# Attention and a mixture of adapters: three score buffers, two shared PSUM banks, casts tied to VectorE steps

## The chip, the cores and the metric

One core of one Trainium2 chip runs the whole kernel. The metric is the device time of one execution in microseconds (us). Engines are named as in the profile: PE is TensorE, DVE is VectorE, ACT is ScalarE, POOL is GpSimd, and SP is SyncE, which here only issues DMAs.

## The reference

Eight batches of eight heads, 576 positions, head size 64. Scores get a bias that depends on the distance of query and key; softmax; then values. The result x, 4608 rows of 512, goes through a gated mixture of eight adapters of rank 16, the best two per row.

```python
scores = scale * np.matmul(q, k.transpose(0, 1, 3, 2))
scores = scores + bias.transpose(2, 0, 1)[None]     # bias_table[bucket(|i - j|)]
attn = np.exp(scores - scores.max(-1, keepdims=True))
attn = attn / (attn.sum(-1, keepdims=True) + 1e-09)
x = np.matmul(attn, v)                              # then rows of all heads side by side
logits = x @ w_gate
w = softmax over the best two logits of a row
out = x + sum over those two e of w[e] * ((x @ A[e]) @ B[e])
```

## The kernel before, in words

The work goes in 32 pairs of heads (`i`, four pairs `hp` per batch `b`). Of the 576 positions 512 are the main part, in four tiles of 128, and 64 are a tail; the tails of the two heads of a pair share one tile. A pair has five score groups `g`: groups 0 to 3 are a key tile against the 512 main queries, for both heads, and group 4 has the tails.

`qk(i, g)` (L316) takes a `sc` tile (two PSUM banks, two buffers), runs the score matmuls (L323, or L327 and L331 for group 4), and has ACT write `exp` of them as bf16 into `p` (L335). The bias comes in as a factor: `band` (L338) multiplies the parts of `p` near the diagonal by exp of the bias, from `M` or `M4`; two heads by 256 or 384 columns at L350 (shown as 128x512 and 128x768), 256 columns at L342 for group 4. `pv(i, sl)` (L355) multiplies all groups with the values for one of five slots of 128 query rows, with a column of ones for the sum. All five slots stand in one tile `pv` of two banks, which has one buffer. `norm` (L380) takes the reciprocal of the sums (L388), a mask for the tail slot (L391), and multiplies 640 columns into `x` (L392).

Ahead of that, `cast_kq` (L122) makes bf16 copies `kqn` of keys and queries, and `cast_v` (L134) of values `vn`, on POOL. `transposes` (L281) turns `kqn` by eight PE transposes into `kqps`, and DVE copies that to `kqT` (L289). The mixture of a batch (`m_*`, L401 to L538) follows its attention: x transposed by a DMA on SP (`m_xdma`, L404), logits (L438), gates on DVE, POOL and ACT (`m_gate`), z (L487), its transpose (L505), outputs (L513), a sum on DVE (L517) and stores on SP (L523, L538). The shared tail tile of two batches has instructions of its own. All PSUM tiles but `sc` and `pv` take turns in two one-bank buffers named `acc`.

The order on every engine is written out by hand. The loop (L587 to L632) goes through pairs and, inside, groups: the scores of group `g` of pair `i`; then transposes for pair `i+1`, mixture steps that `mixture` (L543) has put into `events` at a group's number, values of pair `i-1`, its norm at group 4; and last the band of the group before (`late`). Each engine runs its own instructions in that order. SP takes, in the same order, loads of the next batch (`load_kq`, `load_v`), stores and the transposing DMA. POOL takes tail loads (`load_tails`, `load_vtails`), casts and gate steps. Before the loop (L139 to L255) come the loads of batch 0, with values cast by 16 DMAs from POOL (L152), and the bias: a row `g_sb` made on DVE, its exp `ge` (L189), written to DRAM (L191) and read back as shifted copies `Mr` and `MHr` (L198, L204), from which `bias_pair` (L221) builds `M`, `M4` and `MHT`.

Of the kernel before, what the change touches and what calls it, by code (L numbers as in the profile page):

```python
# [10 lines left out]
FP32 = mybir.dt.float32  # L11
# [16 lines left out]
def kernel(  # L28
# [37 lines left out]
    scp = ctx.enter_context(tc.tile_pool(name="sc_ps", bufs=2, space=PSUM))  # L66
    pvp = ctx.enter_context(tc.tile_pool(name="pv_ps", bufs=1, space=PSUM))
# [3 lines left out]
    make_identity(nc, ident)  # L71

# [3 lines left out]
    def alloc_loads(b):  # L76
        kf = ldp.tile([128, H, 4 * D], FP32, name="kf", tag="kf")
        qf = ldp.tile([128, H, 4 * D], FP32, name="qf", tag="qf")
        kfs[b] = (kf, qf)
        if b > 0:  # L80
            vfs[b] = ldp.tile([128, 4, H, D], FP32, name="vf", tag="vf")
# [25 lines left out]
    def load_tails(b):  # L107
        for w, src in enumerate((k, q)):
            sr = src[b, :, S4:, :].rearrange("(c e) p d -> e p c d", e=2)
            for e in range(2):  # L110
                s = slice(e * 64, (e + 1) * 64)
                nc.gpsimd.dma_start(out=tls[b % 2][s, w, :, s], in_=sr[e])

    def load_vtails(b):
        sr = v[b, :, S4:, :].rearrange("(c e) p d -> e p c d", e=2)
        for e in range(2):
            nc.gpsimd.dma_start(  # L117
                out=vts[b % 2][e * 64:(e + 1) * 64, :, e * D1:e * D1 + D], in_=sr[e])
# [3 lines left out]
    def cast_kq(i, w, eng=None):  # L122
# [8 lines left out]
        else:  # L131
            (eng or nc.gpsimd).tensor_copy(o, s)  # L132

    def cast_v(i):  # L134
        b, hp = divmod(i, HP)
        h = slice(2 * hp, 2 * hp + 2)
        nc.gpsimd.tensor_copy(vns[b % 2][:, :, h, :D], vfs[b][:, :, h, :])  # L137

    alloc_loads(0)  # L139
    load_kq(0, 0, 2)  # L140
    btT = cp.tile([H, NB], FP32, tag="btT")
    nc.sync.dma_start(out=btT, in_=bias_table.rearrange("b h -> h b"))
    for t in tls[:1] + vts[:1]:
        nc.vector.memset(t, 0.0)
    load_kq(0, 2, 4)
    load_kq(0, 4, 6)
    load_tails(0)

    nc.vector.memset(vns[0][:, :, :, D:D1], 1.0)
    for j in range(4):  # L150
        for t in range(4):
            nc.gpsimd.dma_start(  # L152
                out=vns[0][j * 32:(j + 1) * 32, t, :, :D],
                in_=v[0, :, t * 128:(t + 1) * 128, :]
                .rearrange("h (p j) d -> j p h d", j=4)[j])
# [5 lines left out]
    nc.vector.memset(g_sb, 0.0)  # L161
    cast_kq(0, 0, nc.vector)
    cast_kq(0, 1, nc.scalar)
    bsub = cp.tile([H, NB], FP32, tag="bsub")
    nc.vector.tensor_scalar(bsub, btT, btT[:, NB - 1:NB], None, op0=ALU.subtract)
# [11 lines left out]
    nc.vector.tensor_copy(g_sb[:, C:C + nsm], bsub[:, :nsm])  # L177
    nc.vector.tensor_copy(
# [3 lines left out]
    for bv, lo, hi in runs[nsm:]:  # L182
# [3 lines left out]
        nc.vector.tensor_copy(dst, bsub[:, bv:bv + 1].unsqueeze(2)  # L186
# [4 lines left out]
    nc.sync.dma_start(out=g_d.ap(), in_=ge)  # L191
# [42 lines left out]

    for t in tls[1:] + vts[1:]:
# [430 lines left out]
```

## Time and profile before

| What | Value |
|---|---|
| Runs | 254.53, 255.85, 285.35 us; median 255.85 |
| Profiled execution | 256.31 us, span 254.5 us |
| PE busy | 187.8 us (74%) |
| DVE busy | 195.0 us (77%) |
| ACT busy | 162.7 us (64%) |
| POOL busy | 117.3 us (46%) |
| Mean granted clock of PE | 0.919 |

The span is the time from the first to the last instruction; what lies around it is not in the profile. Busy shares are means over the span. PE's matmuls are pipelined and overlap in the records, so a busy PE need not be at its peak. In rows of time, the first number is the start and the second the duration, in us, and what stands in brackets is the idle time just before and what ended it. Rows with merged instructions carry a count (x8) and the time from the first start to the last end.

### The profile page before, as it was taken

What the parts mean: (1) busy time and instruction counts of PE and PEld (TensorE: products, weight loads), DVE (VectorE), ACT (ScalarE), POOL (GpSimd) and SP (SyncE); (2) the same over time, 40 slices, a digit from 0 to 9 for tenths busy, and PEclk for the clock granted to TensorE, in tenths of its full rate; (3) what the DMA queues carried; (4) which work ended last, traced back from release to release, by engine and by line L of the source; (5) the groups of instructions that cost most, each with busy time, mean ns of one, the idle gap of its engine ahead of it and who ended that gap; (6) DMA issues with size and microseconds to landing.
All of it is one profiled execution on the core that took longest, in us unless ns stands there. A gap on an engine that the chain in (4) does not pass through costs nothing.

```text
span 254.5 us, 6519 instructions
## 1 busy us (share of the span) xinstructions
PE 187.8 (74%) x2496; PEld 123.7 (49%) x2496; DVE 195.0 (77%) x483; ACT 162.7 (64%) x184; POOL 117.3 (46%) x229
## 2 busy tenths in 40 slices
PE   1324965888987596869879898879784997897650
PEld 1102543655754473546646574547353675556510
DVE  5215673899999579897997698988998599798771
ACT  3251874689987485777876586769676487895000
POOL 8599928671835254334743282714452282020100
PEclk9999998899999889899997797999889599999965
DMA  7999996997988697596987693886967301910616
GB/s 163 148 128 271 273 97 146 308 150 153 322 108 199 135 292 113 128 186 157 324 155 166 166 304 38 183 175 198 244 152 162 74 0 38 213 45 3 165 36 170
DMA packets 91830, 41.28 MB, mean 162 GB/s; under 512 B 69648, under 2 KB 87064, under 8 KB 91800
## 3 DMA queue, kind: packets, MB, share of 16 engines
q1 hardware_dynamic: 74392, 38.77, 61.5%
q0 software_dynamic: 17408, 2.10, 14.8%
q8 instruction: 19, 0.31, 0.5%
q14 instruction: 11, 0.09, 0.1%
HBM read 29.84 MB, written 9.45 MB: 154 GB/s over the span
## 4 chain that ended last, share of the span: by engine, by line
PE 43%; DVE 32%; DMA 13%; POOL 7%; issue 2%; ACT 1%; DVEq 0%; POOLq 0%; ACTq 0%
PE pv L366 17%; DMA xT<-x 11%; PE sc L323 9%; DVE p L350 6%; DVE x L392 6%; DVE o L517 5%; PE zp L487 3%; DVE p L342 3%; DMA tl<-in_q_dram 3%; DVE rm L391 3%; PE dl L513 3%; PE kqps L287 3%; DVE kqT L289 2%; POOL vn L152 2%; DVE tlT L298 2%
## 5 line engine op out<-in xcount | busy, mean ns | idle before, releaser
L335 ACT ACTIVATE p<-sc 128x1024 bf16<-128x1024 f32 x160 | 155.8, 1024 | 65.7 <-PE sc L323 36.1
L366 PE MATMUL pv<-vn,p 128*128 128x65 bf16 (+1 forms) x1152 | 68.2, 206 | 12.6 <-DVE x L392 12.5
L366 PEld LDWEIGHTS <-p 128*128 128x128 bf16 x1280 | 59.0, 104 | 37.4 <-issue 18.9
L350 DVE TENSOR_TENSOR p<-p,M 128x512 bf16<-128x512 bf16 (+1 forms) x128 | 66.2, 533 | 3.3 <-POOL M L223 2.7
L323 PE MATMUL sc<-kqT 64*128 64x512 bf16 x256 | 54.0, 419 | 2.8 <-ACT p L335 2.8
L287 PE MATMUL kqps<-ident,kqn 128*128 128x128 bf16 x256 | 21.6, 229 | 17.0 <-POOL kqn L132 10.0
L366 PE MATMUL pv<-vt,p 128*128 128x130 bf16 x128 | 29.8, 232 | 2.4 <-DVE p L342 2.4
L453 POOL TENSOR_TENSOR df<-lg,m 128x32 f32<-128x32 f32 (+1 forms) x12 | 3.5, 293 | 60.6 <-DVE lg L443 31.8
L287 PEld LDWEIGHTS <-kqn 128*128 128x128 bf16 x256 | 15.8, 101 | 24.6 <-POOL kqn L132 11.3
L392 DVE TENSOR_TENSOR x<-pv,rm 128x640 bf16<-128x640 f32 x32 | 26.4, 825 | 1.1
L289 DVE COPY kqT<-kqps 128x1024 bf16<-128x1024 bf16 x32 | 21.8, 682 | 7.0 <-PE kqps L287 7.0
L117 POOL DMA_DIRECT2D vt<-in_v_dram x16 | 9.8, 621 | 32.6 <-PE pv L366 32.6
L517 DVE TENSOR_TENSOR o<-dl,x 128x512 f32<-128x512 f32 x32 | 21.7, 687 | 3.7 <-PE dl L513 2.7
L323 PEld LDWEIGHTS <-kqT 64*128 64x128 bf16 x256 | 12.8, 94 | 18.5 <-issue 7.3
L132 POOL CAST kqn<-kf 128x512 bf16<-128x512 f32 x31 | 21.1, 680 | 0.1
L132 POOL CAST kqn<-qf 128x512 bf16<-128x512 f32 x31 | 20.5, 662 | 0.0
L137 POOL CAST vn<-vf 128x512 bf16<-128x512 f32 x28 | 20.5, 733 | 0.0
L342 DVE TENSOR_TENSOR p<-p,M 128x256 bf16<-128x256 bf16 x32 | 18.5, 579 | 0.1
L513 PE MATMUL dl<-Bb,zT 128*128 128x512 bf16 x32 | 14.2, 452 | 4.4 <-DVE kqT L289 2.5
L327 PE MATMUL sc<-kqT,tlT 128*128 128x512 bf16 x32 | 13.7, 427 | 0.0
L331 PE MATMUL sc<-tlT,kqT 128*128 128x128 bf16 x128 | 13.5, 233 | 0.0
L438 PE MATMUL lp<-Wb,xT 128*128 128x8 bf16 x128 | 4.5, 167 | 11.9 <-DMA xT<-x 11.9
(85 smaller groups left out, 209.3 us busy)
## 6 DMA issues: line engine op xcount, KB each, us to landing
out_dram<-o SPq DMA_DIRECT2D x64, 128.0 KB, 2.3
kf<-in_k_dram SPq DMA_DIRECT2D x7, 1024.0 KB, 5.9
qf<-in_q_dram SPq DMA_DIRECT2D x7, 1024.0 KB, 10.2
vf<-in_v_dram SPq DMA_DIRECT2D x112, 64.0 KB, 2.9
kf<-in_k_dram SPq DMA_DIRECT2D x4, 256.0 KB, 4.5
qf<-in_q_dram SPq DMA_DIRECT2D x4, 256.0 KB, 4.4
out_dram<-ot SPq DMA_DIRECT2D x8, 128.0 KB, 2.6
tl<-in_k_dram POOLq DMA_DIRECT2D x16, 32.0 KB, 6.8
```

What stands on the lines that cost most here:

```text
L132: (eng or nc.gpsimd).tensor_copy(o, s)
L137: nc.gpsimd.tensor_copy(vns[b % 2][:, :, h, :D], vfs[b][:, :, h, :])
L287: nc.tensor.transpose(o[:, :, j, :], n[:, w, j], ident)
L289: nc.vector.tensor_copy(t, ps)
L323: nc.tensor.matmul(sc[:, h * 512:(h + 1) * 512], lhsT=t[s, 0, g * 128:(g + 1) * 128], rhs=t[s, 1, :], start=True, stop=True)
L335: nc.scalar.activation(p, sc, ACT.Exp, scale=scale)
L342: nc.vector.tensor_tensor(p[:, 384:640], p[:, 384:640], M4[:, hp, :], op=ALU.mult)
L350: nc.vector.tensor_tensor(o, o, Mh[:, :, x0 * 128:(x0 + b1 - b0) * 128], op=ALU.mult)
L366: nc.tensor.matmul(acc[:, sl * SLOT + o:sl * SLOT + o + n], lhsT=lhsT, rhs=rhs, start=start, stop=stop, skip_group_check=True)
L392: nc.vector.tensor_tensor(xs[b][:, :, 2 * hp:2 * hp + 2, :], at(acc, 0, (SLOT, 5), (D1, 2), (1, D)), rm.unsqueeze(3).to_broadcast((128, 5, ...
L513: nc.tensor.matmul(ps, lhsT=zT[:, t, :], rhs=Bb, start=True, stop=True)
L517: nc.vector.tensor_tensor(o[:, t], ps, xs[b][:, t].rearrange("p h d -> p (h d)"), op=ALU.add)
```

## The change

- Score tiles `sc` get three buffers. `qk` only runs matmuls, for group number n (five per pair, counted through); the activation is a function `expo(n)`. The loop issues scores two groups ahead: `qk(n + 2)`, then `expo(n)`.
- The `pv` pool goes. `pv` takes a one-bank `acc` tile for slots 0 to 2 and another for slots 3 and 4. `norm` has two parts, at groups 2 and 4, with a reciprocal each (`recip`); the mask step is two slots wide.
- All DVE instructions go through a `Recorder` that keeps the last one. `behind_dve` makes a POOL cast wait for the last DVE instruction issued before it. In the loop the three casts of a pair stand just ahead of a DVE step that reads PSUM: the copy of `kqT` at group 0, and the two parts of `norm` at groups 2 and 4.
- Head: the bias table is loaded first; batch 0's values are loaded as fp32 by ACT's and SP's queues, and cast on DVE; `ge` is written by ACT's queue; casts for pairs 0 to 2 and bias tiles for pairs 0 and 1 are on DVE. Tail loads are issued one piece at a time.
- Mixture weights are loaded and cast by POOL's DMAs, without POOL casts. Value loads for the next batch go in 2, 1 and 1 pieces at pairs 0, 1 and 2 of a batch.
- Mixture: the tail tile becomes a fifth tile of `xT` and of all steps after it in every second batch; steps are placed at other groups (`mixture`).

```diff
-    scp = ctx.enter_context(tc.tile_pool(name="sc_ps", bufs=2, space=PSUM))
-    pvp = ctx.enter_context(tc.tile_pool(name="pv_ps", bufs=1, space=PSUM))
+    scp = ctx.enter_context(tc.tile_pool(name="sc_ps", bufs=3, space=PSUM))
     acp = ctx.enter_context(tc.tile_pool(name="acc_ps", bufs=2, space=PSUM))
...
+    dve = Recorder(nc.vector)
+
+    def behind_dve(inst):
+        tc.add_manual_dep(
+            inst.ins, dve.last.ins.name,
+            mybir.DependencyInfo(mybir.DependencyClass.Sync,
+                                 mybir.DependencyReason.DATA),
+            reason="reads SBUF beside an instruction with an input in PSUM")
...
     alloc_loads(0)
-    load_kq(0, 0, 2)
     btT = cp.tile([H, NB], FP32, tag="btT")
     nc.sync.dma_start(out=btT, in_=bias_table.rearrange("b h -> h b"))
+    load_kq(0, 0, 2)
+    load_v(0, (0, 1), nc.scalar)
...
+    for w in range(2):
+        for e in range(2):
+            load_tail(0, w, e)
     load_kq(0, 2, 4)
+    load_v(0, (2, 3))
     load_kq(0, 4, 6)
-    load_tails(0)
...
-            nc.gpsimd.dma_start(
-                out=vns[0][j * 32:(j + 1) * 32, t, :, :D],
...
-    nc.sync.dma_start(out=g_d.ap(), in_=ge)
+    nc.scalar.dma_start(out=g_d.ap(), in_=ge)
+    cast_kq(0, 0, dve)
+    cast_kq(0, 1, nc.scalar)
+    cast_kq(1, 0, dve)
+    cast_kq(1, 1, dve)
...
+        k = sl % 3
+        if k == 0:
+            pvs[(i, sl // 3)] = acp.tile([128, 3, 2 * D1], FP32, name="pv", tag="acc")
...
+    def recip(i, part):
+        if i % HP == 0 and part == 0:
+            xs[i // HP] = xp.tile([128, 5, H, D], BF16, name="x", tag="x", bufs=4)
+        n = 3 - part
+        rc = sp.tile([128, n, 2], FP32, name="rc", tag=f"rc{part}")
+        dve.reciprocal(rc, at(pvs[(i, part)], D, (2 * D1, n), (D1, 2)))
+        rcs[(i, part)] = rc
...
         if b < B - 1:
-            at_slot(0, 0, lambda: m_xdma(b))
+            at_slot(0, 4, m_xdma, b)
         else:
+            at_slot(0, 4, m_x, b, 0)
+            at_slot(0, 4, m_x, b, 1)
+        if tail:
+            at_slot(1, 4, m_xtail, b)
+        at_slot(2, 0, m_logits, b)
+        for n in range(4):
+            at_slot(2, (2, 3, 4, 4)[n], m_gate, b, n)
+        at_slot(3, 0, m_z, b, 0, 4)
+        if tail:
+            at_slot(3, 2, m_z, b, 4, 5)
+        at_slot(3, 4, m_zT, b)
+        at_slot(4, 0, m_out, b, 0)
+        at_slot(4, 2, m_out, b, 1)
+        at_slot(5, 0, m_out, b, 2)
+        at_slot(5, 2, m_out, b, 3)
+        if tail:
+            at_slot(6, 4, m_outt, b)
...
+    for n in range(NG + 5):
+        i, g = divmod(n, 5)
         b, hp = divmod(i, HP)
+        nb = b + 1
+        if n + 2 < NG:
+            qk(n + 2)
+        if n < NG:
+            expo(n)
...
+            for j in ((0, 1), (2,), (3,), ())[hp]:
+                load_v(nb, (j,))
+        if g in (1, 3) and hp < 3 and nb < B:
+            load_tail(nb, hp, g // 2)
+        if 10 <= n < 15:
+            load_weights(n - 10)
...
+        if i < HP and g == 2:
+            cast_v(i, dve)
+        if n == 2:
+            bias_pair(0, dve)
+            band(0)
+        if g == 4 and i > 0:
+            mask_tail(i - 1)
+        if 1 < n <= NG:
+            band(n - 1)
...
+        if g == 0 and i + 1 < NPAIR:
+            if 3 <= i + 2 < NPAIR:
+                behind_dve(cast_kq(i + 2, 0))
+            transposes(i + 1)
+        if g == 2 and hp == 2 and nb < B:
+            tail_transposes(nb)
+        if i > 0:
+            if g == 1:
+                pv(i - 1, 0)
+                pv(i - 1, 1)
+            if g == 2:
+                pv(i - 1, 2)
+                recip(i - 1, 0)
+            if g == 3:
+                pv(i - 1, 3)
+                pv(i - 1, 4)
+                recip(i - 1, 1)
+        if g == 2 and 3 <= i + 2 < NPAIR:
+            behind_dve(cast_kq(i + 2, 1))
+        if g == 4 and HP <= i + 1 < NPAIR:
+            behind_dve(cast_v(i + 1))
+        if i > 0 and g in (2, 4):
+            norm(i - 1, g // 2 - 1)
+        for f, a in events.pop(n, ()):
+            f(*a)
```

## Rows read from the trace of the kernel before

**Rows 1.** Windows: us, busy (x) of PE, PEld, DVE, ACT, POOL; clock; DMA share.

```profile
0.00:25.60 25.60, 7.69 (x45) 3.68 (x45) 8.95 (x38) 7.98 (x11) 21.45 (x50) 1.00 1.09 178
25.60:233.50 207.90, 170.13 (x2333) 114.04 (x2332) 173.93 (x413) 154.29 (x172) 94.60 (x174) 0.93 0.77 165
233.50:254.50 21.00, 10.03 (x120) 5.97 (x120) 12.17 (x34) 0.44 (x2) 1.30 (x6) 0.75 0.42 113
```

**Rows 2.** Timeline of PE, the first matmul of group 4 of four pairs.

```profile
95.25 0.38 PE L327 MATMUL sc<-kqT,tlT 128*128 128x512 bf16 x1
104.42 0.38 PE L327 MATMUL sc<-kqT,tlT 128*128 128x512 bf16 x1
225.95 0.38 PE L327 MATMUL sc<-kqT,tlT 128*128 128x512 bf16 x1
230.97 0.38 PE L327 MATMUL sc<-kqT,tlT 128*128 128x512 bf16 x1
```

**Rows 3.** Timeline of SP's queue and PE, x transposed and used.

```profile
136.46 1.80 SPq L404 DMA_TRANSPOSE xT<-x  x1
140.95 0.55 PE L438 MATMUL lp<-Wb,xT 128*128 128x8 bf16 x16 [1.30 <-DMA xT<-x]
```

**Rows 4.** Timeline of DVE, POOL and PE in one long pair.

```profile
96.06 1.87 DVE L350 TENSOR_TENSOR p<-p,M 128x768 bf16<-128x768 bf16 x1
96.84 0.66 POOL L132 CAST kqn<-kf 128x512 bf16<-128x512 f32 x1
98.31 0.61 PE L287 MATMUL kqps<-ident,kqn 128*128 128x128 bf16 x8 [1.30 <-DVE zT L507]
100.26 0.38 PE L513 MATMUL dl<-Bb,zT 128*128 128x512 bf16 x1 [0.96 <-DVE kqT L289]
```

**Rows 5.** Windows, a stretch behind those waits.

```profile
101.00:103.00 2.00, 2.00 (x14) 0.77 (x12) 1.63 (x4) 1.02 (x1) 0.00 (x0) 0.50 0.00 0
```

**Rows 6.** Waits: engine line <- releaser: us in total, times, longest us.

```profile
PE pv L366 <- DVE x L392: 12.5, 13, 1.9
```

**Rows 7.** DVE instructions of three lines: duration in ns, min/median/max.

```profile
L342 DVE TENSOR_TENSOR p<-p,M x32: 279/283/2512, 25.6 to 233.5; 128x256 bf16<-128x256 bf16 x32
L391 DVE TENSOR_TENSOR rm<-rc,mask x32: 152/164/1953, 32.0 to 236.7; 128x10 f32<-128x10 f32 x32
L392 DVE TENSOR_TENSOR x<-pv,rm x32: 824/825/826, 32.6 to 236.9; 128x640 bf16<-128x640 f32 x32
```

**Rows 8.** Groups by form, whole span: xcount | busy us, mean ns | idle.

```profile
L350 DVE TENSOR_TENSOR p<-p,M 128x768 bf16<-128x768 bf16 x64 | 38.4, 609 | 0.6 <-ACT p L335 0.5
L350 DVE TENSOR_TENSOR p<-p,M 128x512 bf16<-128x512 bf16 x64 | 29.3, 458 | 2.7 <-POOL M L223 2.7
L342 DVE TENSOR_TENSOR p<-p,M 128x256 bf16<-128x256 bf16 x32 | 18.5, 579 | 0.1
L391 DVE TENSOR_TENSOR rm<-rc,mask 128x10 f32<-128x10 f32 x32 | 10.2, 319 | 0.0
L388 DVE RECIPROCAL rc<-pv 128x10 f32<-128x10 f32 x32 | 6.8, 212 | 7.2 <-PE pv L366 7.1
```

**Rows 9.** Groups by form, DVE, 226 to 254.5 us, almost without casts.

```profile
L350 DVE TENSOR_TENSOR p<-p,M 128x768 bf16<-128x768 bf16 x3 | 1.6, 548 | 0.0
L350 DVE TENSOR_TENSOR p<-p,M 128x512 bf16<-128x512 bf16 x3 | 1.1, 374 | 0.0
```

**Rows 10.** Timeline of PE with queued work.

```profile
117.06 0.41 PE L366 MATMUL pv<-vn,p 128*128 128x65 bf16 x8
117.36 0.38 PE L327 MATMUL sc<-kqT,tlT 128*128 128x512 bf16 x1
118.18 0.39 PE L323 MATMUL sc<-kqT 64*128 64x512 bf16 x2
```

**Rows 11.** Timeline of the head, SP's queue and POOL.

```profile
12.86 1.75 SPq L198 DMA_DIRECT2D Mr<-g_d  x4
21.79 0.61 POOL L132 CAST kqn<-kf 128x512 bf16<-128x512 f32 x1
```

More of the change, by code (lines that the diff above doesn't have):

```diff
@@ L105, with load_tail @@
         vns.append(vn)
[L107 to L116, printed above, removed]
-            nc.gpsimd.dma_start(
-                out=vts[b % 2][e * 64:(e + 1) * 64, :, e * D1:e * D1 + D], in_=sr[e])
+    def load_tail(b, w, e):
+        sr = (k, q, v)[w][b, :, S4:, :].rearrange("(c e) p d -> e p c d", e=2)
+        s = slice(e * 64, (e + 1) * 64)
+        o = (tls[b % 2][s, w, :, s] if w < 2 else
+             vts[b % 2][s, :, e * D1:e * D1 + D])
+        nc.gpsimd.dma_start(out=o, in_=sr[e])
     kqn = {}
@@ L325, in qk, with expo, band @@
                                  rhs=t[s, 1, :], start=True, stop=True)
[L326 to L333 removed]
+            return
+        tt = tlT[b]
+        nc.tensor.matmul(sc[:, 0:512], lhsT=tt[:, 0, hp, :], rhs=t[:, 1, :],
+                         start=True, stop=True)
+        for j in range(4):
+            o = 512 + TPOS[j] * 128
+            nc.tensor.matmul(sc[:, o:o + 128], lhsT=t[:, 0, j * 128:(j + 1) * 128],
+                             rhs=tt[:, 1, hp, :], start=True, stop=True,
+                             skip_group_check=True)
+    def expo(n):
+        i, g = divmod(n, 5)
         p = pp.tile([128, 2 * S4], BF16, name=f"p{g}", tag=f"p{g}")
[L335 removed]
+        nc.scalar.activation(p, scs.pop(n), ACT.Exp, scale=scale)
         probs[(i, g)] = p
[L338 removed]
+    def band(n):
+        i, g = divmod(n, 5)
         b, hp = divmod(i, HP)
@@ new lines, in recip, with mask_tail @@
+    def recip(i, part):
[5 more added lines that the diff above has]
+        rcs[(i, part)] = rc
+    def mask_tail(i):
+        rm = sp.tile([128, 2, 2], FP32, name="rm", tag="rm")
+        dve.tensor_tensor(rm, rcs[(i, 1)], mask, op=ALU.mult)
+        rcs[(i, 1)] = rm
@@ L398, with norm, tiles, new_xT @@
+    def norm(i, part):
+        b, hp = divmod(i, HP)
+        n = 3 - part
+        dve.tensor_tensor(xs[b][:, 3 * part:3 * part + n, 2 * hp:2 * hp + 2, :],
+                          at(pvs.pop((i, part)), 0, (2 * D1, n), (D1, 2), (1, D)),
+                          rcs.pop((i, part)).unsqueeze(3)
+                          .to_broadcast((128, n, 2, D)), op=ALU.mult)
     st = {}
+    def tiles(b):
+        return 4 + b % 2
+    def new_xT(b):
+        st[(b, "xT")] = xp.tile([128, 20, 128], BF16, name="xT", tag="xT")
@@ L415, in m_x @@
                                 ident)
[L416 removed]
+        dve.tensor_copy(st[(b, "xT")][:, half * 8:half * 8 + 8, :], ps)
     def m_xtail(b):
[L420 removed]
         ps = acp.tile([128, 4, 128], FP32, name="xtps", tag="acc")
@@ L633 @@
-    for key in sorted(events):
-        for f in events[key]:
-            f()
+        nb = b + 1
[3 more added lines that the diff above has]
+            expo(n)
+        if g == 0 and nb < B:
+            if hp == 0:
+                alloc_loads(nb)
+                load_kq(nb, 0, H)
+            for j in ((0, 1), (2,), (3,), ())[hp]:
[4 more added lines that the diff above has]
+            load_weights(n - 10)
@@ new lines @@
+        if g == 0 and 1 <= i < HP - 1:
+            bias_pair(i + 1, nc.gpsimd)
+        if i < HP and g == 2:
[7 more added lines that the diff above has]
+            band(n - 1)
+        if g == (4 if b == 0 else 1) and hp == 0 and i < NPAIR:
+            tail_scores(b)
+        if g == 4 and hp == 0 and i < NPAIR:
+            tail_band(b)
+        if n == 1:
+            tail_transposes(0)
```

327 lines of the change are left out of this document (114 added, 213 removed).

## The prediction

> **What bounds the kernel now.** I read the busy table by stretch first. It has a head (to 25.6 us, where pair 0's last band begins), a middle of 207.9 us (to pair 31's last band) and a tail of 21.0 us [rows 1]. The middle holds 31 pair steps, so a pair costs 207.9 / 31 = 6.71 us. In it VectorE (DVE) is busy 173.93 us (84%), ScalarE (ACT) 154.29 (74%), and no engine is full. So the loss changes from pair to pair, and the next view is the timeline at one mark per pair, the first matmul of group 4 on TensorE (PE). The 31 gaps between marks fall into three sorts: 12 are under 5.8 us (the last, 225.95 to 230.97, is 5.02), 12 lie between 5.9 and 7.3, and 7 are above 8.5 (95.25 to 104.42 is 9.17) [rows 2]. What makes a pair long is therefore worth more than what any engine needs for one.
>
> Three of the seven hold a wait for x: the transposing DMA goes out at 136.46, and PE takes its result at 140.95 after idle time [rows 3]. SP issues in order, and value loads and output stores stand ahead of that DMA. Another three look like the one from 95.25, where GpSimd (POOL) runs casts back to back, and a DVE band multiply begun at 96.06 lasts 1.87 us. DVE, late by then, empties PSUM late: PE waits 1.30 us for a shared bank at 98.31 and 0.96 at 100.26 [rows 4]. Behind that the granted clock is at 0.50, the lower level of 1.2 GHz, for 101 to 103 [rows 5]. The seventh lies in the first batch.
>
> One loss runs through many pairs: PE waits for the normalisation to leave the only `pv` buffer, 12.5 us in 13 waits [rows 6]. And what POOL does to DVE shows in the spread: the 256-column band takes 0.279 us at least and 2.512 at most, the mask step 0.152 to 1.953, but the multiply with an input in PSUM (L392) 824 to 826 ns in all 32 cases [rows 7]. On that difference the change rests.
>
> **The change, part by part.** I take the pair's cost on each engine after the change, and let the largest set the pace.
>
> *DVE.* Hold-ups that can go, as means less undisturbed durations: 64 x (0.609 - 0.548) + 64 x (0.458 - 0.374) + 32 x (0.579 - 0.279) + 32 x (0.319 - 0.152) = 3.9 + 5.4 + 9.6 + 5.3 = 24 us [rows 7 to 9]. Added: a second reciprocal per pair, 31 x 0.212 = 6.6 us [rows 8]. The normalisation in two parts reads the same 640 columns, with a second fixed cost between nothing and a small instruction, 0.21; I take 0.15, 4.7 us in all. Four key/query casts, four value casts and one pair's bias copies move to DVE; POOL takes 0.66 for such a cast [rows 4]; at half that to all of it 3 to 7 us, partly in the head; I take 3 in the middle. The fifth tile joined to the other four saves some 15 small instructions, 2 us. So 173.9 - 24 + 6.6 + 4.7 + 3 - 2 = 162 us, 5.2 us a pair.
>
> *ACT.* Its work stays: 154.29 / 31 = 5.0 us a pair at most [rows 1]. With three score buffers PE may write group n+2 while group n is read, so ACT can run on for two groups without PE. Its waits for scores are late PE, and vanish as far as PE keeps up.
>
> *PE.* From starts of queued work: a value slot 0.30 (117.06 to 117.36), group 4's scores and slot 4 together 0.82 (117.36 to 118.18) [rows 10]. By columns (512 in that slot's eight 65-wide and one 130-wide matmul take 0.30, with the weight loads) a score group is about 0.3, eight key/query transposes about 0.45, a batch's mixture about 4 us. Four slots, four groups, 0.82, 0.45 and 1.0 make 4.7 us a pair at full clock.
>
> *What is put in the way.* The two-bank `pv` tile goes. Its halves, 3 and 2 slots, use two banks in turn with everything else: key/query transposes, tail tiles, logits, z, outputs, about 5.6 uses a pair. PE must not write a use before DVE has emptied the use two back. PE is in order, so behind that wait stand the next scores, and ACT waits for them once its two groups are gone; DVE then finds no band to multiply. I walked one pair with two output tiles by these durations: transposes written by 0.7 us, copied by 1.4, first half written 1.5 to 2.3, normalised by 3.9, second half written 4.0 to 4.7, normalised by 6.0. In it DVE idles once, 0.3 us. So two banks cost from nothing to 1.0 us a pair (a third of the 3.0 us that PE spends writing into them); I take 0.2, near that walk.
>
> *The tie.* Each cast waits for the DVE step before a PSUM step: the key cast runs beside the copy of `kqT` (1024 columns), the query cast beside 3/5 and the value cast beside 2/5 of the normalisation (about 0.55 and 0.4 us, from 0.825 for the whole [rows 7]). A cast of 0.66 may outlast the last two by 0.1 to 0.3, and a band that comes then is held. Cost 0 to 0.4 us a pair; I take 0.2. Behind a waiting cast on POOL stand tail loads, later casts and the gate steps. A cast has three groups of lead or more, about 3 us, before PE transposes its tile, so nothing late is expected; without that lead PE would idle as at the start, where pair 1's cast is late [rows 11].
>
> *SP, and the long pairs.* The weights go from SP's queue to POOL's, batch 0's value loads from POOL's to SP and ACT, and a later batch's value loads leave in 2, 1 and 1 pieces over three pairs. x's DMA stands just behind the end of the normalisation and the logits six groups later, 6.6 us, against 4.5 from issue to use [rows 3]; loads of the next batch can go out before. That takes away the first sort of long gap, the tie the second. What is left I take at about 1 us a batch, within the rounding.
>
> A pair: 5.2 + 0.2 + 0.2 = **5.6 us**. Ends: 5.0 (ACT) and 6.6 (the 5.2 with both dear ends).
>
> *Head and tail.* Pair 0's bias tiles wait on DMAs through DRAM, which SP issues at 12.86; pair 1's cast on POOL begins only at 21.79, behind 16 value DMAs that POOL issues [rows 11]. That cast moves to DVE. So pair 0's last band could begin at 20 instead of 25.6 (bounds: 17, if the bias row is written 3 us sooner too, and 25.6, if nothing is gained). The tail, a chain of the same steps, stays at 21.0 (plus or minus 2): two outputs come later in it, other steps sooner.
>
> The head's loads share DMA engines that are at 1.09 of their time there [rows 1]. The Trainium skill says in "DMA: Bandwidth & Descriptors", section "Issuing engines are not separate DMA queues", that DMAs of ScalarE, SyncE and GpSimd run on the same 16 engines, so that another issuer saves only the issue time. By that rule alone the head stays at 25.6, and the sum is 222. POOL's late cast is no matter of bandwidth, which is why I go lower.
>
> The profiled run took 256.31 us for a span of 254.5, so 1.8 lie outside. Sum: 20 + 31 x 5.6 + 21.0 + 1.8 = 216.4, say **216 us**. That run is 0.2% above the median of 255.85; no correction.
>
> **Rivals.**
> *Banks partly chained, or the tie does nothing.* Banks at 0.7 a pair, or half of the 24 us still there and long gaps with them: 6.1, so 20 + 189 + 22.8 = 232 us. For it: only two tiles lie between two engines of about 5 us each. Against: the walk.
> *Long pairs stay.* x still comes late behind stores on SP, or late emptying still drops the clock: seven gaps at 9 and 24 at 5.5, 195 + 42.8 = 238 us. For it: SP is still in order. Against: the loads can run ahead.
> *ACT's pace.* Small DVE instructions overlap and all pairs go at 5.0: 155 + 42.8 = 198 us. For it: the last gap is 5.02 [rows 2].
> *Slower: PE and DVE take turns on the two banks.* If no write overlaps emptying, a pair costs DVE's 5.2 plus the 3.0 us that PE writes into these banks, 8.2: 254 + 42.8 = 297 us. It decides from (256.3 - 42.8) / 31 = 6.9 us a pair, when 1.7 of the 3.0 are uncovered. For it: waits of this sort exist at 98.31 and 100.26 [rows 4], and now `pv` shares those banks. Against: they came behind a held band, and uses alternate.
> *The clock.* If waits on banks keep PE at 1.2 GHz, its 4.7 us double to 9.4 a pair: 291 + 42.8 = 334 us. For it: the 0.50 behind two such waits [rows 5]. Against: over the whole middle, with all its waits, the mean is 0.93 [rows 1]. The Trainium skill has this rule in "TensorE: Matmul & The Clock Gate", section "A second HAM failure mode: psum-queue depth-cycling": cycling through PSUM banks makes PE idle briefly and its clock swing, which speaks against the change. The trace agrees on one stretch and not on the mean.
>
> **How the numbers follow.** Chances: forecast 0.50, 232 us by either way 0.22, long pairs 0.12, ACT's pace 0.06, turns 0.06, clock 0.04. The range runs from 201 (head 17, 5.2 a pair) to 239, past both middle rivals; left out are ACT's pace, turns, clock and strays, under 0.2. A measurement of this kernel can tell about 2% from no change, so 251 to 261 is within. Faster holds forecast, ACT and nearly all of the middle rivals, 0.87; within 2%, 0.05 (strays of the middle rivals and the start of turns); slower 0.08 (the rest of turns and the clock).
>
> **What would show it.** Right: gaps between marks of 5.3 to 5.9 with none above 7; ACT over 85% busy in the middle; the 256-column band always near 0.28 and the mask step near 0.16; clock near 1.0; pair 0's last band at 20. Wrong: waits of PE on DVE's copies of over 1.5 us a pair (turns); the wait for x before the logits, or stretches at 0.50 (long pairs); bands above 1 us beside casts (the tie); pair 0's last band at 25 (head).

## The result, and the profile after

The changed kernel takes 241.46 us (median of 4 runs, 238.83 to 242.86) against 257.74 us for the kernel before beside it: ratio 0.939, 95% interval 0.922 to 0.955. It is faster, by 6%. The forecast was 216 us with a range of 201 to 239: the sign was right, the size was not; some 16 us were gained where 40 were promised. The profiled execution took 242.86 us for a span of 241.1. The ratio is that of the fast runs alone (254.53 and 255.85 us before, 240.34 and 238.83 after), and the profiled execution is the slowest of the four.

The windows of the same three stretches as in [rows 1], and of four pairs that nothing disturbs, from pair 12's mark to pair 16's (us; busy and count of PE, PEld, DVE, ACT, POOL; clock; DMA share; GB/s):

```profile
0.00:21.80 21.80, 8.99 (x55) 4.46 (x55) 12.00 (x42) 8.67 (x11) 9.83 (x29) 1.00 0.93 192
21.80:219.10 197.30, 162.21 (x2320) 109.40 (x2320) 164.56 (x470) 151.11 (x169) 91.42 (x163) 0.95 0.89 177
219.10:241.10 22.00, 11.74 (x120) 7.03 (x121) 12.12 (x31) 0.24 (x1) 0.80 (x3) 0.67 0.41 108
...
94.64:118.52 23.88, 20.64 (x308) 13.79 (x306) 21.71 (x62) 19.61 (x23) 11.55 (x21) 1.00 0.81 165
```

Read DVE against the length of the middle. Before, it was idle for 207.9 - 173.93 = 34.0 us; now for 197.30 - 164.56 = 32.7. So the change took 9.4 us out of DVE's work and almost nothing out of its idle time. The forecast had put the work at 162 us, nearly what it is, and the idle time at 0.4 us a pair, 12.4 us. That difference, 20.3 us, is most of the error of 26.5.

The marks, as in [rows 2] (first matmul of group 4, now issued two groups ahead):

```profile
94.64 0.38 PE L339 MATMUL sc<-kqT,tlT 128*128 128x512 bf16 x1
100.48 0.38 PE L339 MATMUL sc<-kqT,tlT 128*128 128x512 bf16 x1
...
118.52 0.38 PE L339 MATMUL sc<-kqT,tlT 128*128 128x512 bf16 x1
124.36 0.38 PE L339 MATMUL sc<-kqT,tlT 128*128 128x512 bf16 x1
134.75 0.63 PE L339 MATMUL sc<-kqT,tlT 128*128 128x512 bf16 x1
```

Four even pairs take 23.88 us, 5.97 each, at full clock. The pair from 124.36 takes 10.39, and its last mark has a matmul of 0.63 us instead of 0.38: the lower clock. In the first batch the gaps are 5.08, 7.51 and 10.22. The excess over the forecast's span of 214.6 us comes apart as follows (a rest of 0.4 us lies between marks and bands):

| Part | Forecast | Measured | Excess, us |
|---|---|---|---|
| Head, to pair 0's last band | 20 | 21.8 | 1.8 |
| Three gaps of the start | 3 x 5.6 | 22.81 | 6.0 |
| Even level of the other 28 gaps | 5.6 | 5.97 | 10.4 |
| Long pairs among these 28 (sum 174.88) | none | 174.88 - 28 x 5.97 | 7.7 |
| Tail | 21.0 | 22.0 | 1.0 |

The tie does on DVE what it was meant to. All DVE lines stand at the recorder's line, so they are told apart by tile and form, as in [rows 8]:

```profile
L82 DVE TENSOR_TENSOR p<-p,M 128x768 bf16<-128x768 bf16 x64 | 36.2, 567 | 0.0
L82 DVE TENSOR_TENSOR p<-p,M 128x512 bf16<-128x512 bf16 x64 | 27.6, 432 | 0.0
L82 DVE TENSOR_TENSOR p<-p,M 128x256 bf16<-128x256 bf16 x32 | 12.4, 388 | 0.0
```

And min/median/max of the mask step and of the two-slot normalisation, as in [rows 7]:

```profile
L82 DVE TENSOR_TENSOR rm<-rc,mask x32: 161/164/250, 26.3 to 222.4; 128x4 f32<-128x4 f32 x32
L82 DVE TENSOR_TENSOR x<-pv,rm x32: 410/418/424, 26.7 to 222.6; 128x256 bf16<-128x256 f32 x32
```

The 256-column band went from 579 to 388 ns, the mask step's longest from 1953 to 250. By the prediction's own formula 64 x 0.019 + 64 x 0.058 + 32 x 0.109 + 32 x 0.015 = 8.9 us of hold-ups are left of 24. That x is still late shows on SP's queue and PE, as in [rows 3]:

```profile
114.71 8.07 SPq L114 DMA_DIRECT2D vf<-in_v_dram  x8
123.42 2.69 SPq L542 DMA_DIRECT2D out_dram<-o  x4
126.22 2.99 SPq L432 DMA_TRANSPOSE xT<-x  x1
...
132.50 0.70 PE L465 MATMUL lp<-Wb,xT 128*128 128x8 bf16 x20 [3.64 <-DMA xT<-x]
```

x was normalised at 122.6. Eight value loads for the next batch hold SP until 122.8, four stores until 126.1, and only then does the transposing DMA go out. It takes 6.3 us to its use, and PE stands for 3.64. Waits of PE and DVE over the whole span (total, times, longest):

```profile
DVE rc L82 <- PE pv L380: 9.8, 26, 0.8
...
PE lp L465 <- DMA xT<-x: 7.3, 3, 3.6
...
PE pv L380 <- DVE x L82: 5.8, 16, 0.7
...
PE tps L306 <- DMA tl<-in_q_dram: 3.7, 1, 3.7
PE dl L532 <- DVE x L82: 3.0, 6, 0.5
```

Where one wait of [rows 6] had 12.5 us, with single ones of 1.9, PE and DVE now wait for each other's `pv` in many small pieces, none above 0.8 us. The two waits for DMAs are few and long.

### The profile page after: what moved, and what is told of

Its sections match the earlier page's. It is cut to its first block, busy times and chain, and to the rows that moved or that the text cites. A ratio compares the mean times of both kernels' runs of the same rounds, so it can differ in the third digit from the quotient of the medians.

```text
span 241.1 us, 6561 instructions
## 1 busy us (share of the span) xinstructions
PE 182.9 (76%) x2492; PEld 120.9 (50%) x2496; DVE 188.7 (78%) x540; ACT 160.0 (66%) x180; POOL 102.0 (42%) x195
## 4 chain that ended last, share of the span: by engine, by line
DVE 34%; PE 31%; DMA 20%; SPq 4%; issue 4%; POOL 2%; ACT 1%; POOLq 0%; DVEq 0%
PE pv L380 14%; DVE p L82 9%; DVE x L82 8%; DMA xT<-x 8%; DVE o L82 5%; DMA vf<-in_v_dram 4%; DVE kqT L82 3%; DMA tl<-in_q_dram 3%; PE sc L334 3%; DVE rc L82 3%; PE sc L343 2%; PE sc L339 2%; DMA kf<-in_k_dram 2%; PE zp L511 2%; DMA qf<-in_q_dram 2%
## 5 line engine op out<-in xcount | busy, mean ns | idle before, releaser
L350 ACT ACTIVATE p<-sc 128x1024 bf16<-128x1024 f32 x160 | 152.2, 1038 | 24.6 <-PE pv L380 11.5
L82 DVE TENSOR_TENSOR p<-p,M 128x512 bf16<-128x512 bf16 (+2 forms) x160 | 73.9, 477 | 0.0
L380 PE MATMUL pv<-vn,p 128*128 128x65 bf16 (+1 forms) x1152 | 61.4, 201 | 11.1 <-DVE x L82 5.8
L380 PEld LDWEIGHTS <-p 128*128 128x128 bf16 x1280 | 53.8, 101 | 26.7 <-issue 14.5
L334 PE MATMUL sc<-kqT 64*128 64x512 bf16 x256 | 49.8, 409 | 1.6 <-DVE kqT L82 0.8
L152 POOL CAST vn<-vf 128x512 bf16<-128x512 f32 x28 | 17.3, 620 | 31.0 <-DVE p L82 19.8
L82 DVE RECIPROCAL rc<-pv 128x6 f32<-128x6 f32 x64 | 11.8, 184 | 9.9 <-PE pv L380 9.8
L82 DVE TENSOR_TENSOR x<-pv,rc 128x384 bf16<-128x384 f32 x32 | 17.8, 558 | 1.1
L82 DVE COPY tlT<-tps 128x1024 bf16<-128x1024 bf16 x8 | 5.5, 692 | 10.4 <-PE tps L306 10.3
L82 DVE TENSOR_TENSOR x<-pv,rm 128x256 bf16<-128x256 f32 x32 | 13.3, 417 | 0.0
```

Source lines behind the costliest of these rows:

```text
L82: self.last = f(*a, **kw)
L152: return (eng or nc.gpsimd).tensor_copy(vns[b % 2][:, :, h, :D], vfs[b][:, :, h, :])
L334: nc.tensor.matmul(sc[:, h * 512:(h + 1) * 512], lhsT=t[s, 0, g * 128:(g + 1) * 128], rhs=t[s, 1, :], start=True, stop=True)
L350: nc.scalar.activation(p, scs.pop(n), ACT.Exp, scale=scale)
L380: nc.tensor.matmul(acc[:, k, o:o + n], lhsT=lhsT, rhs=rhs, start=start, stop=stop, skip_group_check=True)
```

## The experiments

The theory formed from this profile has three parts: (a) two shared banks cost more than the 0.2 us a pair of the forecast; (b) transfers that come late make the long pairs; (c) DVE's hold-ups were dear in busy time but not on the path. The rivals: the tie carries the whole gain; the third score buffer does; DVE sets the pace alone. Ratios are to the kernel before, run on the same chip (its medians were 254.05 to 256.36 us). Where two intervals overlap, as those of the changed kernel and e3_v_late do, the totals alone do not tell the two apart, and the traces are read beside them.

**The tie.** Without it:

```diff
     def behind_dve(inst):
+        return
```

> The changed kernel (median 241.5 us) with the tie alone taken out: casts stand where they stood, but no longer wait for a VectorE step. If the tie is worth what the prediction put on it, most of the 24 us of hold-ups on VectorE come back: the 256-column band has a mean near 0.58 us again, single ones above 2 us, and the time is 255 to 262 us. Rival: the casts are spread over the groups anyway and few meet a band; then bands have a mean under 0.45 and the time is 240 to 246 us.

Measured: 243.92 us, ratio 0.9615 (0.9509 to 0.9721). DVE by form:

```profile
L82 DVE TENSOR_TENSOR p<-p,M 128x768 bf16<-128x768 bf16 x64 | 43.6, 683 | 0.0
L82 DVE TENSOR_TENSOR p<-p,M 128x512 bf16<-128x512 bf16 x64 | 29.8, 466 | 0.0
...
L82 DVE TENSOR_TENSOR p<-p,M 128x256 bf16<-128x256 bf16 x32 | 14.1, 440 | 0.0
...
L82 DVE TENSOR_TENSOR rm<-rc,mask 128x4 f32<-128x4 f32 x32 | 6.9, 216 | 1.2
```

DVE's busy time rises from 188.7 to 200.1 us, 11.4 more, but the time by 2.5 (medians) to 5.8 us (ratios, whose intervals overlap), as the second expectation said. The total hides two effects that work against each other. Windows from pair 8's mark to pair 12's, of the changed kernel and then without the tie, and without it PE's wait for x over the whole span:

```profile
70.46:94.64 24.18, 20.89 (x322) 14.28 (x319) 21.95 (x64) 19.67 (x23) 11.62 (x21) 1.00 0.87 196
...
72.82:97.95 25.13, 21.02 (x323) 14.25 (x320) 24.05 (x65) 19.66 (x23) 12.10 (x21) 1.00 0.84 188
...
PE lp L466 <- DMA xT<-x: 2.5, 3, 1.8
```

The four pairs take 0.95 us more for 2.10 us more of DVE's work, so about half of it arrives there. But PE waits 2.5 us for x instead of 7.3, and no gap behind the first three is above 7.42 us: the slower pairs leave SP's queue time to catch up. What the tie saves in the even pairs, the late DMA takes back. At 0.95 / 4 = 0.24 us a pair the tie would be worth 7 us over 31 pairs if no transfer were late; that is an estimate from these windows, and no run shows it. The counterpart is the kernel before with the tie alone. Its casts move with it, since it has only two PSUM steps a pair to stand beside:

```diff
+                if 1 <= i and i + 2 < NPAIR:
+                    behind_dve(cast_kq(i + 2, 0))
                 transposes(i + 1)
...
+        dve.tensor_tensor(rm, rc, mask, op=ALU.mult)
+        if casts[0] is not None:
+            behind_dve(cast_kq(casts[0], 1))
+        if casts[1] is not None:
+            behind_dve(cast_v(casts[1]))
```

> The kernel before with the tie alone: the key cast of pair i+2 waits for the VectorE step ahead of the copy of kqT, the query cast and the value cast for the mask step, so that they run beside the normalisation's 825 ns. By the prediction's term (24 us of hold-ups on VectorE, all on the path) it would go from 256 to 232 to 240 us. By what e1_no_tie shows (11 us more busy time on VectorE for 2 to 6 us) it gains 3 to 8 us: 248 to 253 us. If the second of two tied casts still holds the band behind the normalisation, nothing is gained: 254 to 258 us.

Measured: 258.36 us, ratio 1.0175 (1.0086 to 1.0263): no gain, rather a loss of under 3%. Two groups of DVE show what the tie did:

```profile
L83 DVE TENSOR_TENSOR p<-p,M 128x256 bf16<-128x256 bf16 x32 | 11.7, 364 | 0.1
L83 DVE TENSOR_TENSOR rm<-rc,mask 128x10 f32<-128x10 f32 x32 | 5.2, 163 | 0.0
```

And two waits, of POOL and of PE, what it cost:

```profile
POOL kqn L156 <- DVE rm L83: 90.6, 27, 5.2
...
PE kqps L311 <- POOL kqn L156: 35.5, 29, 7.6
```

The hold-ups are mostly gone here too (579 to 364 ns, 319 to 163), but the query cast, moved from group 2 to the normalisation, now comes after PE wants it, 29 times for 35.5 us in all. So all three expectations missed, the third by 0.4 us and with another reason; the prediction's remark that a tied cast without its lead leaves PE idle is what happened. This run doesn't price the tie by itself, since the casts also moved.

**More work for DVE.** Two multiplies of 128x256 a pair on a tile that nothing reads, in pairs 4 to 31:

```diff
+        if g in (1, 3) and HP <= i < NPAIR:
+            nc.vector.tensor_tensor(dum, dum, M4[:, 0, :], op=ALU.mult)
```

> The changed kernel with two more VectorE multiplies of 128x256 bf16 (0.28 us each, on a tile of their own) in each of the pairs 4 to 31: 28 x 0.56 = 15.7 us of added VectorE work, nothing waits for it. If VectorE sets the pace of the even stretches (21.7 us busy of 23.9), nearly all of it shows: 253 to 258 us. If the pace is set by waits between PE and VectorE, with slack on VectorE, under half of it shows: 243 to 248 us.

Measured: 247.81 us, with runs from 241.98 to 248.9. The 56 multiplies took 297 ns each, 16.6 us, and the time rose by 3 (lowest runs) to 6 us. In the even stretch four pairs go from 23.88 to 24.68 us: 0.20 of the 0.59 us a pair shows, while DVE's busy time there grows by 0.39 (21.71 to 23.28 us for four). The second expectation holds: DVE alone doesn't set this kernel's pace.

**The banks.** Two score buffers with scores one group ahead, and four shared banks:

```diff
-    scp = ctx.enter_context(tc.tile_pool(name="sc_ps", bufs=3, space=PSUM))
-    acp = ctx.enter_context(tc.tile_pool(name="acc_ps", bufs=2, space=PSUM))
+    scp = ctx.enter_context(tc.tile_pool(name="sc_ps", bufs=2, space=PSUM))
+    acp = ctx.enter_context(tc.tile_pool(name="acc_ps", bufs=4, space=PSUM))
...
-        if n + 2 < NG:
-            qk(n + 2)
+        if n + 1 < NG:
+            qk(n + 1)
```

> The changed kernel with PSUM shared out the other way: two score buffers (scores one group ahead), four shared banks. If PE and VectorE taking turns on two shared banks is what lifts the pair from the forecast 5.6 us to 5.95, PE's waits for copies out of shared banks nearly vanish and the time falls by about 0.3 us in each of 31 pairs, to 230 to 234 us, as long as ACT is not held. If instead the third score buffer is what keeps ACT and VectorE fed, PE waits for ACT's exp at every group and the time rises to 247 to 258 us. I expect the second, weakly: 240 to 252 us.

Measured: 239.92 us, ratio 0.9443 (0.9346 to 0.9539). The time says "no difference" from the changed kernel, just under the weak expectation, but not for its reason: the even pairs are the fastest yet (22.41 us from pair 8's mark to pair 12's, against 24.18 in the changed kernel), while PE's waits for x's DMA rose from 7.3 to 15.7 us. To read it, x's DMA had to be freed first:

```diff
-            for j in ((0, 1), (2,), (3,), ())[hp]:
-                load_v(nb, (j,))
...
+    VL = ((1, 2), (1, 4), (2, 1), (2, 3))
...
+        if nb < B and (hp, g) in VL:
+            load_v(nb, (VL.index((hp, g)),))
```

> The changed kernel with the next batch's value loads moved behind the transposing DMA: none at the first pair of a batch, pieces of four DMAs at groups 2 and 4 of the second pair and 1 and 3 of the third. If SP's queue makes the long pairs (x's DMA issued at 126.22 us, x ready at 122.6), that DMA leaves within 2.5 us of the end of the normalisation, PE's waits for xT (7.3 us) and the clock dips behind them go, and the time is 231 to 236 us. If x's DMA is late by its own length, or the loads now run beside it, the waits stay and the time is 239 to 243 us.

Measured: 236.3 us, ratio 0.931 (0.922 to 0.940). The wait for x fell from 7.3 to 4.7 us, the pair of 10.39 us to 7.38. The DMA goes out at once (x is normalised at 121.43, it leaves at 121.75), but takes 7.3 us to its use, beside other loads and stores; the time lies between the two expectations, nearer the first. Both edits together, and two buffers with two banks to tell the two apart (two PSUM banks unused):

> The changed kernel with four shared banks and two score buffers (as e2_banks) and the next batch's values loaded behind x's DMA (as e3_v_late). The pairs of e2_banks that nothing else disturbed came at 5.48, 4.82, 6.13 and 5.64 us (mean 5.52, against 5.97 in the changed kernel), but x's DMA held one pair of each batch for 3 to 5 us. If two shared banks and SP's queue are two separate losses, both go: 31 x 0.45 = 14 us less than e3_v_late's 236, so 222 to 227 us. If x's DMA is late however it is queued, since the pairs before it are now shorter, the time stays at 233 to 240 us.

> e3_v_late with two score buffers (scores one group ahead) and still two shared banks; two PSUM banks stay unused. It tells the score buffers from the shared banks. If the third score buffer is worth something beside two shared banks, the time is 241 to 250 us and clean pairs are above 6.2 us. If it is worth nothing, clean pairs stay at 5.9 to 6.0 us and the time is within 1.5% of e3_v_late (236.3 us).

Measured: 234.9 us, ratio 0.9267 (0.9212 to 0.9323), and 239.68 us, ratio 0.9413 (0.9198 to 0.9629). Windows from pair 8's mark to pair 12's, in which PE waits for x by 0.8 us at most, first of e3_v_late (three score buffers and two shared banks, as in the changed kernel, which takes 24.18 us here):

```profile
68.87:93.37 24.50, 21.01 (x323) 14.26 (x319) 22.05 (x64) 19.68 (x23) 11.62 (x21) 1.00 0.76 165
```

The same of e12_sc2_acc2 (two score buffers, two shared banks):

```profile
72.79:97.31 24.52, 21.61 (x318) 14.46 (x317) 22.03 (x64) 20.37 (x23) 11.61 (x21) 1.00 0.78 171
```

And of e5_banks_v (two score buffers, four shared banks):

```profile
71.70:93.80 22.10, 20.39 (x316) 14.19 (x317) 21.71 (x63) 19.73 (x23) 11.61 (x21) 1.00 0.80 173
```

DVE's work is nearly the same in all, 21.7 to 22.1 us. With two banks, the third score buffer is worth nothing in these pairs (24.52 against 24.50 us; from pair 12 to 16 it is 23.85 against 23.97), as the second expectation of e12_sc2_acc2 said. The 2 to 3 us between the two versions arise in the first three pairs: pair 3's mark comes at 42.51 us against 40.17. With two score buffers, four banks instead of two are worth (24.52 - 22.10) / 4 = 0.60 us a pair, and then DVE is busy 98% of the time: there it does set the pace. So the change gave the scarce banks to the buffer that needed them less. In the whole run only part of that arrived (4.8 us by the medians of e12_sc2_acc2 and e5_banks_v); PE still waits 10.9 us for x there.

**The late transfers.** All mixture steps behind x's DMA three groups later, with four banks and with two:

```diff
-            events.setdefault(5 * (i0 + di) + g, []).append((f, a))
+            late = 3 if b < B - 1 and f not in (m_xdma, m_xtail) else 0
+            events.setdefault(5 * (i0 + di) + g + late, []).append((f, a))
```

> e5_banks_v with all mixture steps behind the transposing DMA three groups later (last batch excepted), so that x's DMA, which took 7.0 us from issue to use beside the value loads (96.99 to 104.03), has about 10 us. If that DMA's length is what is left of the long pairs, PE's waits for xT (10.9 us) and the half-speed stretches behind them go, no pair behind the first four is above 7 us, and the time falls by 3 to 5 us in each of five batches: 214 to 222 us. If something else in that pair is late (tail tiles, x of the next half), 230 to 236 us.

> e3_v_late (three score buffers, two shared banks) with the mixture three groups later. There PE waits only 4.7 us for xT in all and clean pairs are at 5.97 us, so 230 to 235 us; if two shared banks cost 0.45 us a pair, this stays 10 to 15 us above e9_banks_v_shift. If the shared banks cost nothing and four of them only looked better, it is within 2% of it.

Measured: 229.3 us, ratio 0.9086 (0.8982 to 0.9191), and 234.51 us, ratio 0.9309 (0.921 to 0.9409). With two banks the ratio is that of e3_v_late (0.931 both) although PE no longer waits for x. By the profiles something is gained: the 28 gaps behind the first three sum to 164.8 us against 169.8, of which 2.2 us are lost again behind the last mark; the spans are 231.9 and 234.8 us. With four banks the shift gives 1.8 points. The two differ by 2.2 points (5.7 us), less than the 10 to 15 expected, and PE now waits 11.4 us for the next batch's tail queries, a load for which it waited 3.2 us in e5_banks_v. So e9_banks_v_shift lies between its two expectations, near the second. One step more, the tail tiles' transposes one pair later, with four banks and alone in the changed kernel:

```diff
-        if g == 2 and hp == 2 and nb < B:
+        if g == 2 and hp == 3 and nb < B:
             tail_transposes(nb)
```

> e9_banks_v_shift with the transposes of the next batch's tail tiles one pair later (fourth pair of a batch, not third). In e9_banks_v_shift PE waits 11.4 us in six waits for tail queries, 4.35 us of it in the gap of 13 us at the third mark. If those waits are what is left of long pairs, that gap falls to 8 or 9 us, the gaps of 7.7 to 8.4 us further on to 5.5, and the time is 219 to 224 us. If the pair is late for other reasons (casts, DMA bytes), 227 to 231 us.

> The changed kernel with only the next batch's tail transposes one pair later. If they make the gap of 10.2 us at its third mark, that gap falls to 6 or 7 us and the time by 3 to 4 us, to a ratio of 0.92 to 0.93 of the kernel before (0.939 for the changed kernel). If the casts and DMA bytes of the first pairs set it, the ratio stays at 0.935 to 0.945.

Measured: **226.64 us, ratio 0.8876 (0.8802 to 0.8951)**, and 240.78 us, ratio 0.9439 (0.9361 to 0.9517). The first is the best version of the study, 5% below the changed kernel and 11% below the one before; it lies between its two expectations, 0.4 us under the second. In the second version the mark behind the third gap came at 37.5 us instead of 40.8, as the first expectation said, and the time didn't change, as the second said. Its sixth gap is 10.27 us (7.35 in the changed kernel) and ends at 57.79 against 57.64; SP's queue and PE there:

```profile
50.13 2.98 SPq L432 DMA_TRANSPOSE xT<-x  x1
...
55.66 0.59 PE L465 MATMUL lp<-Wb,xT 128*128 128x8 bf16 x16 [4.77 <-DMA xT<-x]
```

The lead of 3 us was spent waiting for x. Between the start and that point the path goes through transfers, so moving one step only moves the wait. The same holds for the head:

```diff
-    load_v(0, (0, 1), nc.scalar)
...
-    load_v(0, (2, 3))
+    load_v(0, (0, 1, 2), nc.gpsimd)
+    load_v(0, (3,))
...
+    for w in range(2):
+        for e in range(2):
+            load_tail(1, w, e)
...
-        if 10 <= n < 15:
-            load_weights(n - 10)
-        if g == 0 and 1 <= i < HP - 1:
+        if 20 <= n < 25:
+            load_weights(n - 20)
+        if g == 1 and 1 <= i < HP - 1:
             bias_pair(i + 1, nc.gpsimd)
```

> e3_v_late with another head: 12 of batch 0's 16 value DMAs go out on POOL's queue and none on ACT's, so that the row ge is not behind eight DMA issues on ACT (0.74 to 8.53 us); batch 1's tail loads of keys and queries go ahead of the loop; the mixture's weights are loaded ten groups later; POOL's bias copies stand behind a cast. If ACT's issues and the loads' order make the slow start, ge is ready 2 to 3 us sooner, pair 0's last band begins at 18 to 20 us instead of 21.8, the two gaps of 8 to 9 us of the first pairs fall to 6 to 7, and the time is 228 to 232 us. If the bytes of the head's loads set it, the time stays within 1% of e3_v_late: 234 to 238 us.

> e5_banks_v with the head of e7_head: all three edits. If the three losses are separate, 215 to 221 us; if one stands behind another, the better of e5_banks_v and e7_head, 222 to 232 us.

> e9_banks_v_shift with the head of e7_head, two faults of it mended: pair 0's value cast on VectorE stands behind the casts of pair 2 (in e7_head it held VectorE for 4.3 us), and the gate weights are loaded first. If the first pairs are slow because of the order of loads and casts, the three gaps of 7 to 12 us behind the first mark fall to 6 to 7 and the time is 6 to 10 us below e9_banks_v_shift. If the loads' bytes set it, within 2 us of it.

> e13_tails with the head's loads in another order: 12 of batch 0's value DMAs on POOL's queue and none on ACT's, pair 0's value cast three groups later, gate weights first, POOL's bias copies behind a cast. e11_all2 had its third mark at 32.5 us against 36.6 in e9_banks_v_shift. If that lead lasts, 3 to 5 us below e13_tails: 214 to 220 us. If it is lost to the next late load, within 2 us of e13_tails.

Measured: 239.76 us, ratio 0.9448 (0.9375 to 0.9522); 236.29 us, ratio 0.9319 (0.9244 to 0.9395); 229.31 us, with runs from 225.47 to 232.65; 229.67 us, ratio 0.9001 (0.893 to 0.9073). Each of these heads brings the first mark from about 18 to 13 or 14 us, since ACT computes `ge` at 4.6 to 4.7 us instead of 9.9. None of it reaches the end: e7_head is no better than e3_v_late, e8_all than e5_banks_v, e11_all2 than e9_banks_v_shift, e14_all3 than e13_tails. e7_head and e8_all had two faults (a value cast that held DVE for 4.3 us, gate weights loaded late); in e11_all2 and e14_all3 they are mended (`load_weights((n - 11) % 5)` from group 15, the cast at group 5), with the same outcome; e14_all3 leaves out the early tail loads. The runs of e11_all2 spread over 7 us, so that a gain of 2 or 3 us can't be told from none there. Of the two expectations of each, e7_head and e8_all missed both, e11_all2 met the second and e14_all3 missed it by 1 us. Where exactly the lead goes in e14_all3 is not settled; PE waits 8.0 us for x in it, against 3.8 in e13_tails.

**DVE's hold-ups once more**, where DVE does set the pace: e13_tails without the tie.

> e13_tails with the tie taken out. If VectorE's hold-ups were cheap in e1_no_tie because two shared banks left VectorE idle for about 0.5 us a pair, they cost more here, where pairs go at 5.6 us and VectorE is 95% busy: 11 us or more of added busy time, and 7 to 12 us above e13_tails. If they are cheap because the casts are spread, 2 to 4 us above it, as in e1_no_tie.

Measured: 229.35 us, ratio 0.8904 (0.8798 to 0.9011), against 0.8876 with the tie. DVE by form, of e13_tails and then of e16_untied4:

```profile
L82 DVE TENSOR_TENSOR p<-p,M 128x256 bf16<-128x256 bf16 x32 | 15.5, 484 | 0.0
...
L82 DVE TENSOR_TENSOR p<-p,M 128x256 bf16<-128x256 bf16 x32 | 12.1, 379 | 0.0
```

The bands of 768 columns rise from 583 to 655 ns, but those of 256 fall from 484 to 379, so the tie keeps DVE clear less well here than in the changed kernel (388 ns). All of DVE rises only from 190.5 to 195.2 us, not by the 11 us of the expectation, and the time by 1 to 3 us. Windows from pair 8's mark to pair 12's, of e13_tails and e16_untied4:

```profile
65.66:87.11 21.45, 20.11 (x316) 14.41 (x317) 21.16 (x63) 19.71 (x23) 9.97 (x18) 1.00 0.77 164
...
64.63:87.49 22.86, 20.43 (x317) 14.54 (x318) 22.57 (x64) 19.73 (x23) 10.05 (x19) 1.00 0.83 182
```

Here all of the added work arrives, 1.41 us of 1.41; in the next four pairs, where PE waits 1.0 us for x in e13_tails, nothing of 0.34 does (22.58 and 22.61 us). So in the whole time the tie is worth at most some 2% in either version, and whether it is worth more where DVE is fuller stays open.

**What carries the gain.** The span fell by 3.8 us in the head and 10.6 in the middle, and the tail took 1.0 back. Neither rival carries it alone: without the tie 2.5 to 5.8 us of it are lost, and without the third score buffer 2 to 3 (e12_sc2_acc2 against e3_v_late, with intervals that overlap). The split normalisation and the mixture's new order were not run by themselves, so their shares are not shown.

## Why the prediction was wrong, by its own steps

*DVE, 5.2 us a pair: right.* 164.56 / 31 = 5.31. The second reciprocal cost 0.157 us (193 + 176 - 212) where 0.212 was put, the split normalisation 558 + 417 - 825 = 150 ns, as put. 15 of the 24 us of hold-ups went. ACT (151.11 / 31 = 4.87) and PE (20.64 / 4 = 5.16 busy, 4.7 put) were no bound, as forecast. The prediction counts 512 columns for the slot of [rows 10]; its nine matmuls have 8 x 65 + 130 = 650, so its prices by columns are rough. ACT came to 77% of the middle instead of over 85%, since the pairs were longer than its work.

*"What is put in the way", banks 0.2 us a pair: the first step that failed.* The walk of one pair found one wait of 0.3 us; 0.5 to 0.6 us were measured. Four banks instead of two take 0.52 off the changed kernel's pair (24.18 to 22.10 us for four, with one score buffer less) and 0.60 at equal score buffers. The walk used one pair with two output tiles and durations without the small waits in the other direction (DVE's reciprocal waits for `pv` 26 times). The rival "banks partly chained" had 6.1 us a pair, near the measured 5.97. Full turns (8.2 us) were far off.

*The tie, 0.2 us a pair: near.* What it left over stands in DVE's work, as held bands: 8.9 / 31 = 0.29 us a pair. As idle time it is small: with the tie and four banks DVE idles (22.10 - 21.71) / 4 = 0.1 us a pair. Late casts cost PE 2.0 us in two waits at the start of the changed kernel. They cost more where the lead was taken away (e6_before_tie) and, what the prediction did not foresee, where pairs are shorter: in e13_tails PE waits 7.8 us for them in nine waits, without the tie (e16_untied4) 5.2 in five.

*"SP, and the long pairs", put within the rounding: the second step that failed.* It cost 7.7 us: the three waits for x, 7.3 us, lie in the three longest of these pairs. The 6.0 us in the start are late transfers too, at least in part: there PE waits 3.7 us for batch 1's tail queries, issued from POOL and 7.2 us on their way. The prediction saw that loads could go out before x's DMA and took it for a gain; eight of them stand before it on SP's queue, and what goes out then runs beside it. The rival "long pairs stay" named this; it was given 0.12. Both middle rivals came true in part at once, and the forecast treated them as alternatives.

*Hold-ups as path time.* The sum took 24 us out of DVE's work and kept its idle time small. In e1_no_tie and e4_dve_load about half of a change in DVE's work arrives in undisturbed pairs (0.95 of 2.10 us and 0.80 of 1.57), and a fifth to a half in the whole time, since shorter pairs wait longer for x.

*Head 20, tail 21.0.* 21.8 and 22.0, inside their bounds. But `ge` came later, not sooner (9.86 us against 6.69), because ACT first issued eight value loads, and the bias copies were issued at 12.66, against 12.86 before [rows 11]; the gain is from the casts on DVE. On ACT's and SP's queues:

```profile
0.74 7.79 ACTq L114 DMA_DIRECT2D vf<-in_v_dram  x8
8.57 1.28 ACT L200 ACT_TABLE_LOAD   x1 [8.57 <-DMA vf<-in_v_dram]
9.86 0.63 ACT L200 ACTIVATE ge<-g_sb 8x512 bf16<-8x512 f32 x1
...
12.66 1.81 SPq L213 DMA_DIRECT2D Mr<-g_d  x4
```

The four versions with another issuer brought the first mark forward by 4 to 5 us and gained no time that their runs can tell; the DMA share in the changed kernel is 0.93 in the head and, by its windows, 1.34 in the third gap. The Trainium skill's rule in "DMA: Bandwidth & Descriptors", section "Issuing engines are not separate DMA queues", that another issuer saves only the time of issuing and brings no further DMA engines, agrees with these runs, though none tests it alone; the prediction weighed it and went lower.

*The clock.* It stays at 1.00 through the even stretch with all its short waits; it is at the lower level, 0.50, behind the 3.64 us in which PE stands for x:

```profile
132.50:136.50 4.00, 4.00 (x54) 3.27 (x55) 1.71 (x9) 1.81 (x3) 0.91 (x2) 0.50 0.88 205
```

The Trainium skill's rule in "TensorE: Matmul & The Clock Gate", section "A second HAM failure mode: psum-queue depth-cycling", is not borne out by this stretch; one long wait did what many short ones did not.

## What to carry to other kernels

Price the idle time of the engine with most work as carefully as its work: ask what will end each wait once the one you remove is gone, and add up the middle rivals instead of choosing among them. When PSUM is short, give banks to the tiles that two engines hand to each other most often, and test a buffer count in a version in which no transfer is late, since a late DMA hides what the banks are worth, and compare the same pairs in both. A single step made earlier or later gains little while the next transfer in the queue decides; here the larger gain came when loads, consumers and banks were moved together.

## What the runs showed of the hardware

The transposing DMA isn't of one length: from issue to use it took 4.5 us in the kernel before [rows 3], 6.3 in the changed one, 7.0 in e5_banks_v (96.99 to 104.03) and 9.9 in e13_tails, beside other loads and stores: in e13_tails the next batch's keys and queries, issued at 109.92 and 110.56, 9.6 us on their way. There it also held SP's queue for 5.72 us. SP's queue and PE in e13_tails:

```profile
114.11 5.72 SPq L432 DMA_TRANSPOSE xT<-x  x1
...
123.97 0.66 PE L465 MATMUL lp<-Wb,xT 128*128 128x8 bf16 x20 [2.03 <-DMA xT<-x]
```

Eight issues of value loads kept ACT from any work for 7.8 us. That is not ACT's own slowness: each issue took 0.32 to 0.51 us, about what SP's issues of key and query loads took (0.43 to 0.47), and the rest is time between them, whose reason no run shows. Eight of the same loads took SP as long, 7.96 us from the first to the last beside ACT's eight, and 8.07 at 114.71.
